# Hashed attention and a two-layer MLP on one core: all queues in a written order from the third chunk on

## The chip, the cores and the metric

The kernel runs on one core of a Trainium2 chip. Times are device microseconds of one execution. A core has five engines with queues of their own: TensorE (PE in the profile, with its weight loads as PEld), VectorE (DVE), ScalarE (ACT), GpSimd (POOL) and SyncE (SP, which here only issues DMAs). An instruction starts when those ahead of it in its queue have gone and when the semaphores it waits for have been raised.

## The reference

Inputs are q, k, v of 4 batches, 8 heads, 768 rows and 64 columns, a projection of 64 x 6, a norm's gain of 512, and two weights of 512 x 2048 and 2048 x 512.

```python
q_bits = einsum('bhsd,dk->bhsk', q, proj) > 0          # 6 bits, k likewise
mask = q_bucket[:, :, :, None] == k_bucket[:, :, None, :]
scores = where(mask, scale * q @ k.T, -1e9)
attn = softmax(scores)                                  # with + 1e-9 in the denominator
x = (attn @ v).transpose(0, 2, 1, 3).reshape(4, 768, 512)
xn = (x - mean) / sqrt(var + 1e-6) * g_ln
out = x + relu(xn @ w_ch1) @ w_ch2
```

## The kernel before

**Chunks.** The output is made in 12 chunks of 256 rows: three for each of four batches, counted here from 0. Chunk n of the loop (line 843) does three things side by side: attention of chunk n, the norm and the first products ("ups", line 559: eight steps of 8 matmuls of 256 columns, L566) of chunk n-1, and the second products ("downs", line 602: eight steps of 4 matmuls of 512 columns, L607) of chunk n-2. Chunks 0 and 1 are in an opening whose order is written out word by word (line 720, `first_two`).

**Attention** of a chunk is 12 units (line 406): four score matmuls (L435), one exponential over 1024 columns on ScalarE (L445), eight value matmuls (L469), and after every third unit a division on VectorE (L487 to L497; from batch 1 on L489, L490, L495, L497). The hash bits are six more rows of the score product, so that unequal buckets fall to nearly nothing.

**MLP.** `norm` (line 532) does statistics and `xn` on VectorE (L516 to L518), then issues from SyncE the DMA that transposes `xn` to `xnT` (L538), then takes the inverse root on GpSimd (L529, L530). In chunk 2 alone `xnT` is made by TensorE and a VectorE copy (`xtrans`, L550, L557). Each up ends with a rectifier, on VectorE and ScalarE in turns (L576, L578). The fourth down of a row block ends with the last sum on VectorE (L612) and the store from SyncE (L616).

**Preparation** of batches 1 to 3 is cut into halves of four heads. A word such as `H20` is step H of batch 2, half 0:

- `L`: loads of q and k (L138, four DMAs on SyncE); `W`: load of v (L157).
- `Q`: four squares on ScalarE for a check of magnitudes (L180), written over the loaded data.
- `N`: q and k to bf16 on GpSimd (L282, two casts into `nat16`, a tile with one buffer).
- `T`: SyncE transposes `nat16` by DMA into `slots` (L304), then moves half of the rows (L309).
- `B`: four block transposes on VectorE (L287) into `bt`; `H`: 32 recorded hash matmuls (L318) that read them, two VectorE instructions (L326, L329), and five DMAs on SyncE (L331, four times L333) that put the bits into `slots`.
- `V`: values to bf16 and their sums, all on GpSimd (L344, L351, L353); `E`: one matmul that shares the sums (L358) and a copy on VectorE (L359).

**What sets the order.** `interleave` (line 678) traces, for each unit, the scores and the exponential of the next unit, then fillers, then the unit's value matmuls and division, then fillers; how many fillers is paid by their costs in the code (a down 870, an up 900, a hash 1300, everything on no PE time 0). In before, the fillers are the norm, the preparation steps of `plan` spread evenly by `mixed` between the downs, then the ups. Only ScalarE keeps this traced order (line 862): for the other four queues Tile's scheduler takes the traced order as a wish, and orders each chunk's instructions by its own priorities and costs. `no_sync_barrier` (line 844) keeps chunks apart in that scheduling.

**Buffers.** PSUM has two banks for the tag `mm`, which ups, downs, hashes, shares and `xtrans` use in turn; two score buffers; two for values. `xn`, `xnT`, `h`, `nat16`, `vnat` and `vs16` have one buffer each.

Of the kernel before, what the change touches and what calls it, by code (L numbers as in the profile page):

```python
# [30 lines left out]
def kernel(  # L31
# [14 lines left out]
    B, H, S, D = q.shape  # L46
# [8 lines left out]
    NT = NC // TT  # L55
# [603 lines left out]

    flag = consts.tile([1, 1], I32)  # L660

    def safety():
        m = work.tile([P, 2], F32, tag="m", name="m")
        nc.vector.tensor_reduce(m, sq, axis=AX.X, op=AOP.max)
        mp = ps_mm.tile([1, 2, P], F32, tag="mm", name="mp")
        for a in range(2):
            nc.tensor.transpose(mp[:, a, :], m[:, a : a + 1], identf)
        m2 = work.tile([1, 2], F32, tag="m2", name="m2")
        nc.vector.tensor_reduce(m2, mp, axis=AX.X, op=AOP.max)
        pr = work.tile([1, 1], F32, tag="pr", name="pr")  # L670
        nc.vector.tensor_mul(pr, m2[:, 0:1], m2[:, 1:2])

        nc.vector.tensor_scalar(
            flag, pr, scalar1=(SAFE_SCORE / scale) ** 2, scalar2=None, op0=AOP.is_le
        )


    def interleave(units, fillers, after=None, single=()):

        total = sum(c for c, _ in fillers) or 1
        slots_n = 2 * len(units)
        done, fi = 0.0, 0

        def fill(upto):
            nonlocal done, fi
            while fi < len(fillers) and done <= upto * total:
                c, f = fillers[fi]
                f()  # L690
                done += c
                fi += 1

        for u, (_, _, values, divide) in enumerate(units):
            nxt = units[u + 1] if u + 1 < len(units) else after
            if nxt:
                nxt[0]()
                nxt[1]()
            fill((2 * u + 1) / slots_n)
            if u % 2 and u // 2 < len(single):  # L700
                for _, f in single[u // 2]:
                    f()
            values()
            divide()
            fill((2 * u + 2) / slots_n)
        while fi < len(fillers):
            fillers[fi][1]()
            fi += 1

    chunks = [(b, t) for b in range(B) for t in range(NT)]  # L710
    preps = [Prep(b) for b in range(B)]
    prep = preps[0]
    def chunk_tile():
        return work.tile([P, TT, d_model], F32, tag="x", bufs=3, name="x")
# [18 lines left out]
    def first_two():  # L733
# [75 lines left out]

    plan = {
        2: "H10 N11 B11 V10 W11 | T11 H11 E10 V11 W20",
        3: "E11 N20 B20 | T20 H20",
        4: "V20 W21 B21 N21 | T21 H21 E20",
        5: "V21 W30 | E21",
        6: "V30 W31 N30 B30 | T30 H30 E30",
        7: "V31 B31 N31 | T31 H31 E31",
    }
    singly = {  # L820
        2: "Q00 L20", 3: "Q01 L21", 4: "Q10 L30", 5: "Q11 L31",
        6: "Q20", 7: "Q21", 8: "Q30", 9: "Q31",
    }

    def prepare(text):
        return [
            step
            for op in text.split()
            for step in preps[int(op[1])].part(op[0], half=int(op[2]))
        ]  # L830

    def mixed(a, b):

        tagged = [((i + 1) / (len(a) + 1), 0, i, s) for i, s in enumerate(a)]
        tagged += [((i + 1) / (len(b) + 1), 1, i, s) for i, s in enumerate(b)]
        return [s for *_, s in sorted(tagged, key=lambda e: e[:3])]

    with tc.manual_schedule():
        first_two()
# [2 lines left out]
    tail = mlp[0][2]  # L842
    for n in range(2, len(chunks)):
        tc.no_sync_barrier()
        mlp[n - 1] = mlp_steps(*chunks[n - 1], xs[n - 1])
        norm, ups, downs, xtrans, _ = mlp[n - 1]
        early, late = (prepare(part) for part in (plan.get(n, "") + "|").split("|")[:2])
        fillers = [norm]
        fillers += mixed(early, tail[:4]) + ([(600, xtrans)] if n == 2 else [])
        fillers += mixed(late, tail[4:]) + ups  # L850
        tail = downs
        if n == NT * (B - 1):
            fillers.append((0, safety))
        after = None
        if n + 1 < len(chunks):
            xs[n + 1] = chunk_tile()
            units[n + 1] = att_units(*chunks[n + 1], xs[n + 1])
            after = units[n + 1][0]
        single = [[step] for step in prepare(singly.get(n, ""))]
        if len(single) > 4:  # L860
            single[3:] = [sum(single[3:], [])]
        with tc.manual_schedule(engines={mybir.EngineType.Activation}):
            interleave(units[n], fillers, after, single)
    tc.no_sync_barrier()
    norm, ups, downs, _, parts = mlp_steps(*chunks[-1], xs[len(chunks) - 1])
# [190 lines left out]
```

## Time and profile before

| what | value |
|---|---|
| median of 3 runs | 321.92 us (320.11 to 322.66) |
| profiled execution, its time | 323.21 us |
| its span, first to last instruction | 320.6 us |
| mean granted TensorE clock | 0.986 |
| PE busy | 304.3 us, 95% of the span |
| ACT, DVE, POOL busy | 216.7, 183.6, 84.8 us |
| chain that ended last | PE 83%, DVE 8%, DMA 4% |

The span is what the trace covers; 2.6 us of the profiled execution's time lie around it. Busy TensorE time counts pipelined matmuls, so 95% doesn't mean that TensorE runs at its peak; the granted clock and the length of like matmuls say more.

### The profile page before, as it was taken

What the parts mean: (1) busy time and instruction counts of PE and PEld (TensorE: products, weight loads), DVE (VectorE), ACT (ScalarE), POOL (GpSimd) and SP (SyncE); (2) the same over time, 40 slices, a digit from 0 to 9 for tenths busy, and PEclk for the clock granted to TensorE, in tenths of its full rate; (3) what the DMA queues carried; (4) which work ended last, traced back from release to release, by engine and by line L of the source; (5) the groups of instructions that cost most, each with busy time, mean ns of one, the idle gap of its engine ahead of it and who ended that gap; (6) DMA issues with size and microseconds to landing.
All of it is one profiled execution on the core that took longest, in us unless ns stands there. A gap on an engine that the chain in (4) does not pass through costs nothing.

```text
span 320.6 us, 7837 instructions
## 1 busy us (share of the span) xinstructions
PE 304.3 (95%) x3268; PEld 227.9 (71%) x3268; DVE 183.6 (57%) x404; ACT 216.7 (68%) x272; POOL 84.8 (26%) x110
## 2 busy tenths in 40 slices
PE   6979999999969997999999999999999999999993
PEld 6566687578648765868868868769769679687563
DVE  1799987634753672465597585535543633635421
ACT  4677976677656674779778778688779667565020
POOL 3467522950330180056064040010200200200200
PEclk9999999999997997999999999999999999999998
DMA  7999996887477489653983533020030110200302
GB/s 241 362 199 302 209 340 103 159 195 197 143 143 215 118 200 177 192 154 133 237 138 90 102 85 86 2 68 34 2 85 15 33 69 0 67 35 0 101 0 76
DMA packets 64970, 40.94 MB, mean 128 GB/s; under 512 B 47152, under 2 KB 59952, under 8 KB 64928
## 3 DMA queue, kind: packets, MB, share of 16 engines
q1 hardware_dynamic: 60224, 31.59, 39.9%
q0 software_dynamic: 4128, 8.13, 10.8%
q10 hardware_dynamic: 576, 0.66, 0.6%
q8 instruction: 27, 0.44, 0.6%
q14 instruction: 15, 0.12, 0.1%
HBM read 27.98 MB, written 6.88 MB: 109 GB/s over the span
## 4 chain that ended last, share of the span: by engine, by line
PE 83%; DVE 8%; DMA 4%; ACT 2%; issue 1%; POOL 0%; SPq 0%; ACTq 0%; POOLq 0%
PE hp L566 27%; PE o L607 21%; PE sc L435 17%; PE av L469 10%; DMA xnT<-xn 3%; PE hash L318 2%; DVE xn L518 2%; DVE slots L262 2%; PE tpose L200 1%; DVE slots L238 1%; DVE bt L287 1%; PE o L589 1%; PE hash L252 1%; DMA knat<-in_k_dram 1%; DVE stats L516 1%
## 5 line engine op out<-in xcount | busy, mean ns | idle before, releaser
L445 ACT ACTIVATE ex<-sc,expb 128x1024 bf16<-128x1024 f32 x144 | 159.4, 1113 | 65.6 <-PE sc L435 63.1
L566 PE MATMUL hp<-xnT,w_sb 128*128 128x256 bf16 x768 | 101.2, 277 | 5.5 <-DMA xnT<-xn 5.2
L607 PE MATMUL o<-w_sb,hbuf 128*128 128x512 bf16 x368 | 92.9, 379 | 0.9 <-DVE x L612 0.8
L435 PE MATMUL sc<-slots 70*128 70x256 bf16 x576 | 87.1, 273 | 2.0 <-POOL slots L238 1.5
L566 PEld LDWEIGHTS <-w_sb 128*128 128x128 bf16 x768 | 72.9, 99 | 15.9 <-DMA xnT<-xn 6.3
L576 DVE TENSOR_SCALAR hbuf<-hp 128x512 bf16<-128x512 f32 x48 | 33.1, 690 | 59.4 <-PE hp L566 59.2
L469 PEld LDWEIGHTS <-ex 128*128 128x128 bf16 x1152 | 54.5, 98 | 15.8 <-ACT ex L445 1.3
L435 PEld LDWEIGHTS <-slots 70*128 70x128 bf16 x576 | 52.0, 97 | 17.1 <-issue 3.7
L469 PE MATMUL av<-vaug,ex 128*128 128x65 bf16 x1152 | 59.3, 194 | 0.3 <-ACT ex L445 0.2
L607 PEld LDWEIGHTS <-hbuf 128*128 128x128 bf16 x368 | 34.0, 97 | 26.8 <-issue 1.1
L529 POOL TENSOR_SCALAR rs<-mv 128x2 f32<-128x2 f32 x12 | 5.6, 471 | 144.2 <-DVE mv L517 144.0
L578 ACT ACTIVATE hbuf<-hp 128x512 bf16<-128x512 f32 x48 | 28.5, 594 | 19.7 <-PE hp L566 19.7
L612 DVE SCALAR_TENSOR_TENSOR x<-o,rs,x 128x512 f32<-128x512 f32 x23 | 17.0, 741 | 31.8 <-PE o L607 31.8
L497 DVE TENSOR_TENSOR x<-x,rc 128x256 f32<-128x256 f32 x36 | 19.0, 528 | 0.9
L282 POOL CAST nat<-qnat 128x1536 bf16<-128x1536 f32 x6 | 9.4, 1570 | 37.5 <-DMA qnat<-in_q_dram 25.5
L518 DVE SCALAR_TENSOR_TENSOR xn<-x,mv,gbc 128x512 bf16<-128x512 f32 x24 | 18.4, 790 | 0.1
L516 DVE BATCH_NORM_STATS2 stats<-x 128x6 f32<-128x512 f32 x24 | 15.4, 681 | 0.3
L490 DVE TENSOR_TENSOR x<-av,vsum 128x256 f32<-128x256 f32 x36 | 14.9, 414 | 0.0
L489 DVE TENSOR_SCALAR rc<-av 128x4 f32<-128x4 f32 x36 | 5.7, 157 | 15.7 <-PE av L469 15.7
L344 POOL CAST vaug<-vnat 128x1536 bf16<-128x1536 f32 x8 | 11.9, 1493 | 7.6 <-PE av L469 4.0
L180 ACT ACTIVATE knat<-knat 128x768 f32<-128x768 f32 x16 | 13.4, 835 | 0.0
L180 ACT ACTIVATE qnat<-qnat 128x768 f32<-128x768 f32 x16 | 13.3, 833 | 0.0
(86 smaller groups left out, 219.8 us busy)
## 6 DMA issues: line engine op xcount, KB each, us to landing
out_dram<-x SPq DMA_DIRECT2D x23, 256.0 KB
vnat<-in_v_dram SPq DMA_DIRECT2D x7, 768.0 KB
qnat<-in_q_dram SPq DMA_DIRECT2D x11, 384.0 KB
knat<-in_k_dram SPq DMA_DIRECT2D x11, 384.0 KB
w_sb<-in_moe_w_ch_dram POOLq DMA_DIRECT2D x4, 1024.0 KB, 14.2
slots<-slots SPq DMA_DIRECT2D x6, 384.0 KB
qnat<-in_q_dram POOLq DMA_DIRECT2D x2, 768.0 KB, 14.7
knat<-in_k_dram POOLq DMA_DIRECT2D x2, 768.0 KB, 16.0
```

The source lines that it names most:

```text
L180: nc.scalar.activation(src, src, AF.Square, accum_out=sq[:, a, col : col + 1],)
L435: nc.tensor.matmul(sc[:, i, :], key_block(h, kj), query_blocks(h),)
L445: nc.scalar.activation(ex, sc, AF.Exp, bias=expb[:, 1:2] if b else expb[:, 0:1], scale=scale if b else scale / Q_SCALE,)
L469: nc.tensor.matmul(av[:, h - ha, qi, :], state[g][:, i, qi * P : (qi + 1) * P], va[:, h, kj, :], start=(b > 0 and (g, i, qi) == (0, 0, 0)) ...
L497: nc.vector.tensor_tensor(xv, num, rc.unsqueeze(3).to_broadcast([P, 2, TT, D]), op=AOP.mult)
L516: nc.vector.bn_stats(stats, x[:, i, :])
L518: nc.vector.scalar_tensor_tensor(xn[:, :, i, :], x[:, i, :].rearrange("p (o d) -> p o d", d=P), mv[:, i, 0:1], gbc.rearrange("p (o d) -> p ...
L566: nc.tensor.matmul(hp[:, i, :], w1_sb[:, dt, nt * P : (nt + 1) * P], st["xnT"][:, dt, :], start=(dt == 0), stop=(dt == ND - 1),)
L576: nc.vector.tensor_scalar_max(dst, src, 0.0)
L578: nc.scalar.activation(dst, src, AF.Relu)
L607: nc.tensor.matmul(o2, st["h"][:, nt, i * P : (i + 1) * P], w2_sb[:, nt, :], start=(nt == 0), stop=(nt == NH - 1),)
L612: nc.vector.scalar_tensor_tensor(x[:, i, :], o2, st["rs"][:, i : i + 1], x[:, i, :], op0=AOP.mult, op1=AOP.add,)
```

## The change

The diff replaces `plan` and `mixed` by `steps`, one string for each of chunks 2 to 8 and 10; other chunks use `plain`. In a string `n` is the norm, `d` and `u` are the next down and the next up, `x` is `xtrans`; each `N` or `B` stands for one of the two casts or four block transposes, and other words for whole preparation steps. The check of magnitudes (`safety`) is cut in two, `m` and `s`, and goes from the end of chunk 9 into chunk 10. And `manual_schedule()` without a list of engines makes all five queues keep the traced order.

```diff
-    plan = {
-        2: "H10 N11 B11 V10 W11 | T11 H11 E10 V11 W20",
-        3: "E11 N20 B20 | T20 H20",
-        4: "V20 W21 B21 N21 | T21 H21 E20",
-        5: "V21 W30 | E21",
-        6: "V30 W31 N30 B30 | T30 H30 E30",
-        7: "V31 B31 N31 | T31 H31 E31",
-    }
+    steps = {
+        2: "n d d H10 d d x N11 d N11 d T11 V10 d W11 d B11 u B11 u B11 u B11 u H11 u E10 u V11 u u",
+        3: "n d d d N20 d N20 B20 E11 d T20 d B20 W20 d d B20 u B20 u H20 u u u u u u",
+        4: "n d d d N21 d N21 B21 d T21 d B21 d d B21 u B21 V20 u H21 u u u W21 u u u",
+        5: "n d d d E20 V21 d d d d d u u u W30 u u E21 u u u",
+        6: "n d d d N30 d N30 B30 d T30 d B30 d d B30 u B30 V30 u H30 u u u W31 u u u",
+        7: "n d d d N31 d N31 B31 E30 d T31 d B31 d d B31 u B31 V31 u H31 u u u u u u",
+        8: "n d d d E31 d d d d d u u u u u u u u",
+        10: "n d d d d m d d d d u u u s u u u u u",
+    }
+    plain = "n d d d d d d d d u u u u u u u u"
...
+    def sequence(text, norm, downs, ups, xtrans):
...
-        fillers = [norm]
-        fillers += mixed(early, tail[:4]) + ([(600, xtrans)] if n == 2 else [])
-        fillers += mixed(late, tail[4:]) + ups
+        fillers = sequence(steps.get(n, plain), norm, tail, ups, xtrans)
...
-        with tc.manual_schedule(engines={mybir.EngineType.Activation}):
+        with tc.manual_schedule():
             interleave(units[n], fillers, after, single)
```

The words of `singly` (squares `Q` and loads `L`) stay between the units where they were. After the loop the last norm, downs and ups are traced as before.

More of the change, by code (lines that the diff above doesn't have):

```diff
@@ L660, with row_maxima, safety @@
     flag = consts.tile([1, 1], I32)
-    def safety():
+    def row_maxima():
         m = work.tile([P, 2], F32, tag="m", name="m")
         nc.vector.tensor_reduce(m, sq, axis=AX.X, op=AOP.max)
+        return m
+    def safety(m):
         mp = ps_mm.tile([1, 2, P], F32, tag="mm", name="mp")
@@ L823, with prepare @@
     }
[L825 to L836, printed above, removed]
+    parts_left = {}
+    def prepare(op):
+        kind, b, half = op[0], int(op[1]), int(op[2])
+        return preps[b].part(kind, half)
+    def sequence(text, norm, downs, ups, xtrans):
+        downs, ups, out = list(downs), list(ups), []
+        for word in text.split():
+            if word == "n":
+                out.append(norm)
+            elif word == "d":
+                out.append(downs.pop(0))
+            elif word == "u":
+                out.append(ups.pop(0))
+            elif word == "x":
+                out.append((600, xtrans))
+            elif word == "m":
+                out.append((0, lambda: parts_left.__setitem__("m", row_maxima())))
+            elif word == "s":
+                out.append((100, lambda: safety(parts_left["m"])))
+            elif word[0] in "BN":
+                if word not in parts_left:
+                    parts_left[word] = prepare(word)
+                out.append(parts_left[word].pop(0))
+            else:
+                out += prepare(word)
+        assert not downs and not ups
+        return out
     with tc.manual_schedule():
@@ L846 @@
         norm, ups, downs, xtrans, _ = mlp[n - 1]
-        early, late = (prepare(part) for part in (plan.get(n, "") + "|").split("|")[:2])
-        fillers = [norm]
-        fillers += mixed(early, tail[:4]) + ([(600, xtrans)] if n == 2 else [])
-        fillers += mixed(late, tail[4:]) + ups
+        fillers = sequence(steps.get(n, plain), norm, tail, ups, xtrans)
         tail = downs
-        if n == NT * (B - 1):
-            fillers.append((0, safety))
         after = None
@@ L858 @@
             after = units[n + 1][0]
-        single = [[step] for step in prepare(singly.get(n, ""))]
+        single = [[step] for op in singly.get(n, "").split() for step in prepare(op)]
         if len(single) > 4:
             single[3:] = [sum(single[3:], [])]
-        with tc.manual_schedule(engines={mybir.EngineType.Activation}):
+        with tc.manual_schedule():
             interleave(units[n], fillers, after, single)
```

## The prediction

> **What bounds the kernel now.** I read the page first: TensorE is busy 95% of the span and is 83% of the chain that ended last. So only two things can move the time: moments in which TensorE waits, and stretches in which it runs slower. The busy time cut at the chunks' borders (a chunk begins with the scores of its second unit) shows where these are. Columns: length, then busy us and instruction counts of PE, PEld, DVE, ACT, POOL, then the granted clock, the DMA share, GB/s. Rows are chunks 2 to 7.
>
> ```profile
> 51.80:79.00 27.20, 26.41 (x319) 19.71 (x317) 15.60 (x28) 18.48 (x25) 14.05 (x16) 1.00 0.69 155
> 79.00:107.80 28.80, 25.84 (x280) 19.00 (x277) 14.93 (x33) 18.35 (x25) 7.46 (x7) 0.94 0.60 155
> 107.80:135.40 27.60, 25.60 (x278) 18.81 (x275) 15.76 (x35) 18.41 (x25) 7.48 (x9) 0.94 0.80 188
> 135.40:157.70 22.30, 22.30 (x248) 17.14 (x245) 12.79 (x29) 18.19 (x25) 9.92 (x11) 1.00 0.56 179
> 157.70:181.50 23.80, 23.80 (x279) 17.95 (x276) 17.53 (x35) 18.32 (x25) 9.10 (x10) 1.00 0.75 131
> 181.50:205.30 23.80, 23.80 (x279) 17.95 (x275) 15.22 (x35) 18.32 (x25) 3.28 (x5) 1.00 0.26 58
> ```
>
> From chunk 5 on TensorE never stops and the clock is 1.00: 22.3 us, and 23.8 with a hash (1.44 us) and a share (0.1). Chunks 3 and 4 hold that same work and take 28.8 and 27.6, at a clock of 0.94. Who TensorE waited for (total, times, longest):
>
> ```profile
> PE hp L566 <- DMA xnT<-xn: 5.2, 3, 2.9
> PE o L607 <- DVE x L612: 0.8, 1, 0.8
> ```
>
> The first is the first up waiting for its transposed input, in chunk 3, in chunk 4 and at the kernel's end. The second falls in chunk 2. Why `xnT` is late stands in SyncE's own order (start, length):
>
> ```profile
> 88.52 3.71 SPq L304 DMA_TRANSPOSE slots<-nat  x1
> 92.34 1.26 SPq L538 DMA_TRANSPOSE xnT<-xn  x1
> ...
> 114.86 3.67 SPq L304 DMA_TRANSPOSE slots<-nat  x1
> 118.63 1.26 SPq L538 DMA_TRANSPOSE xnT<-xn  x1
> ```
>
> `xn` of chunk 3 was done at 83.8 (L518, 83.07 + 0.74), but the scheduler put `T20` ahead of it, and `T20` waited for the GpSimd casts until 88.5 and held the queue until 92.2. TensorE then shows the price twice:
>
> ```profile
> 95.45 1.05 PE L566 MATMUL hp<-xnT,w_sb 128*128 128x256 bf16 x8 [2.88 <-DMA xnT<-xn]
> 96.33 0.41 PE L469 MATMUL av<-vaug,ex 128*128 128x65 bf16 x8
> 96.58 0.74 PE L435 MATMUL sc<-slots 70*128 70x256 bf16 x4
> 97.11 1.92 PE L566 MATMUL hp<-xnT,w_sb 128*128 128x256 bf16 x8
> ```
>
> A wait of 2.88 us, and then an up of 1.92 instead of 1.04: after each of the two waits the granted clock drops for a few us. The wait of 0.80 in chunk 2 is followed by full speed. So a short wait costs itself, a long one about 1.7 us more (chunk 3 loses 5.0 with 2.9 of wait; chunk 4 loses 3.8 with 2.0; the excess is 2.1 and 1.8, part of it issue).
>
> **The change, queue by queue.** In chunks 8 to 11 the traced order of before already is what TensorE ran, so nothing changes there except `safety`.
>
> *SyncE.* `n` comes first, so `xnT` leaves ahead of `T`, of the bits' five DMAs and of the loads. Chunk 5 shows what such an order gives: its first down starts at 135.85, L538 at 139.56, its first up at 146.56, without a wait. From issue to the first up that read it took 3.1 us in chunk 3 (92.34 to 95.45), so 3.9 us are spare. What now stands behind `xnT` (`T` 3.7, L309 0.7 after its landing, five bit DMAs 0.4 + 3.05 and their landing, the stores 0.4 each, four loads 0.5 each) feeds the slots and values of the next batch or half, which are wanted half a chunk later or more. In chunk 2, `H11` is after the loads `L20`; its bits are wanted by unit 6 of chunk 3, some 9 us into it, and I count them there by about 82 us of the span against 88. Gain: 28.8 - 23.8 = 5.0 in chunk 3, 27.6 - 23.8 = 3.8 in chunk 4. Both are whole, wait and clock.
>
> *VectorE, chunk 2.* The 0.80 came from the last sum L612 behind four block transposes (4 x 0.9). These go behind the downs, so L612 follows its down. Gain 0.8.
>
> *Hashes (`H20`, `H21`, `H30`, `H31`).* Each moves from the downs to behind the second up. Its matmuls cost the same 1.44 wherever they are. But the last two block transposes move too, and in VectorE's fixed order the fourth is behind a rectifier and a division. From the end of the last down TensorE reaches the hash after 0.44 + 0.87 + 0.25 + 0.44 + 0.87 + 0.25 = 3.1 us, and after half of the hash, at 3.9, needs the fourth transpose. VectorE is there after 0.2 (release: in chunk 5 a down's values follow it at 140.68, L612 starts at 140.88) + 0.63 (L612 to the next start, 115.18 to 115.81) + 0.89 (third transpose) + 0.63 (rectifier) + 1.03 (division, 101.55 to 102.58) + 0.94 (fourth) = 4.3. So a new wait of 0.4. No row of before has it; below it is 0 if VectorE runs ahead, above it is 1.6 by the longest L497 seen, 1.635 instead of 0.42:
>
> ```profile
> 166.28 1.58 DVE L497 TENSOR_TENSOR x<-x,rc 128x256 f32<-128x256 f32 x1
> ```
>
> That one lay beside a GpSimd cast from 166.13 to 167.59, and `V` (cast 1.5, sums 3.3) runs in this place in chunks 4, 6 and 7, though GpSimd starts it early, behind the casts of `N`. I take 0.55 each, near the lower end: 4 x 0.55 = 2.2 lost. What is late next is the second score block behind it; ScalarE has 1.4 us of hash to catch up in.
>
> [...]
>
> *Shares.* In chunks 3 and 7 a share stands between the last down of one row block and the first of the next. It takes the second `mm` bank, so the down must wait for L612 to empty the first: 0.2 + 0.75 after the fourth down, less 0.36 of values and share, 0.6. Nearest row: the 0.80 above. Bounds 0 and 0.8; I take 0.65 x 2 = 1.3.
>
> *The rest at nothing.* `N`, `V`, `W`, `E20`, `E21` and `V31` go later. GpSimd is busy for 7.5 us in chunk 3 and idle for up to 20.7 us at a time (the longest wait of L529), which hides them; their results are for the batch after. Without that cover a late `N` only delays `T`, no longer `xnT`. If a load lands late, VectorE's `B` blocks what is behind it; before, `L20` was issued at 77.5 and its third piece landed at 85.5; now it goes from about 70, when its last square is done, so there are 5 us to spare. `m` and `s` (two transposes of TensorE, 0.38, and four small VectorE instructions) only change place; uncovered they cost some 1 us (0.38 and four of about 0.16, as L495 takes). Each queue holds as many instructions as before.
>
> *Sum.* 5.0 + 3.8 + 0.8 - 2.2 - 1.3 = 6.1 us. Of the profiled execution: span 320.6 to 314.5, time 323.2 to 317.1. The median of the runs is 1.3 below that execution: **315.8 us**.
>
> **Rivals.**
> (a) *No new wait.* VectorE and the banks keep up: 321.9 - 9.6 = 312.3. For it: VectorE is busy only 15 to 17 of 24 us. Against it: the two orders above.
> (b) *SyncE is late again.* Loads now come late in a chunk, just ahead of the next `xnT`. For it: `T30`, issued right behind loads, held SyncE for 7.39 us instead of 3.7, as much as the spare 3.9. Against it: I count the loads out by the time the norm is done. If half of the 8.8 comes back: 321.9 - 0.8 - 4.4 + 3.5 = 320.2.
> (c) *Slower: hash behind VectorE.* Same place as my 0.55, but divisions or rectifiers wait for GpSimd casts and sums and each hash waits 1.6 or more, with the clock drop of 1.7: 4 x 3.3 = 13.2, and 321.9 - 9.6 + 13.2 + 1.3 = 326.8. It decides from 2.1 us per hash on (8.3 in four), which needs the drop. For it: the 1.58 row, a fixed order. Against it: waits up to 0.8 show no drop, and `V` should mostly be over by then.
> [...]
> (d) *It doesn't do what it says*: some order stays or a wait of another kind eats it; 321.9.
>
> **How the numbers follow.** Forecast 0.50, (a) 0.18, (b) 0.09, (c) 0.17, (d) 0.06. A measurement of this kernel tells about 1%, 3.2 us, from no change. Faster by more (under 318.7): forecast and (a), with a little of the forecast's tail moved over, 0.67. Within 1%: (b), (d) and that tail, 0.16. Slower: (c), 0.17. The range runs from 312.0, just under (a), over the forecast's own ends (0 to 1.0 per hash, 0 to 0.8 per share: 312.3 to 317.9), (b) and (d), to 322.5; only most of (c) is out.
>
> **What would show it.** Right: chunks 3 and 4 at 24 to 25 us with clock 1.00; L538 within 4 us of each chunk's start and ahead of L304; TensorE's waits for `xnT` only the last 0.35; waits of half a microsecond of L318 for L287 and of L607 for L612. Wrong: a wait of 2 us or more anywhere from chunk 2 to 7 with the clock below 1.00, above all at L318, or L566 still waiting for L538.

## The result and the profile after

The changed kernel is slower: 325.86 us median against 321.72 of the kernel before (20 runs each), ratio 1.0119 with a 95% interval of 1.0086 to 1.0153. (The ratio leaves out runs more than 1.5% above the quickest of their kernel, so it isn't quite the quotient of the medians.) The profiled execution of after took 322.48 us, span 319.8, 3.4 us under its median; that of before lay 1.5 us above its own. So the two traces differ by a gain of 0.8 us in span, where the medians differ by a loss of 4.1. The trace of after shows one stall of the kind that costs the time; what fills the other 3.4 us of the median is in no trace of the changed kernel.

Busy time by chunk of that execution, chunks 2 to 7, columns as before:

```profile
52.50:78.78 26.28, 26.12 (x316) 19.77 (x317) 15.40 (x28) 18.48 (x25) 9.20 (x11) 1.00 0.55 124
78.78:103.65 24.87, 24.43 (x277) 18.26 (x276) 16.87 (x33) 18.04 (x25) 9.20 (x10) 1.00 0.69 179
103.65:128.59 24.94, 24.24 (x276) 18.02 (x275) 16.06 (x34) 18.15 (x25) 9.16 (x10) 1.00 0.70 151
128.59:155.35 26.76, 24.25 (x246) 18.20 (x245) 12.01 (x30) 18.37 (x25) 6.21 (x8) 0.94 0.67 201
155.35:179.59 24.24, 24.09 (x276) 18.10 (x275) 15.61 (x34) 18.04 (x25) 9.19 (x10) 1.00 0.43 98
179.59:204.53 24.94, 24.28 (x277) 18.21 (x276) 17.14 (x35) 18.04 (x25) 9.19 (x10) 1.00 0.52 119
```

Chunks 2, 3 and 4 gained 0.9, 3.9 and 2.7 us, chunks 6 and 7 lost 0.4 and 1.1: about as forecast. Chunk 5, which took 22.3 without a stop in before, takes 26.8 at a clock of 0.94, 4.5 us more. What TensorE waited for:

```profile
PE hp L566 <- DMA xnT<-xn: 3.2, 3, 2.3
PE o L607 <- DVE x L612: 0.9, 2, 0.6
```

The wait for `xnT` was not removed; it moved from chunks 3 and 4 to chunk 5 (2.35 us there, 0.59 left in chunk 4). SyncE's order ahead of it:

```profile
124.53 1.59 SPq L331 DMA_DIRECT2D bits_d<-bits  x1
128.58 3.06 SPq L333 DMA_DIRECT2D slots<-bits_d  x4
131.74 0.44 SPq L138 DMA_DIRECT2D qnat<-in_q_dram  x1
132.29 0.40 SPq L138 DMA_DIRECT2D knat<-in_k_dram  x1
132.74 1.45 SPq L138 DMA_DIRECT2D qnat<-in_q_dram  x1
134.25 0.47 SPq L138 DMA_DIRECT2D knat<-in_k_dram  x1
134.81 0.41 SPq L157 DMA_DIRECT2D vnat<-in_v_dram  x1
135.33 2.44 SPq L538 DMA_TRANSPOSE xnT<-xn  x1
```

`xnT` does come ahead of `T` now. But the loads written at the end of chunk 4 stand behind L333, which waits for the bits to land in DRAM (issued at 124.53, read back from 128.58). So five loads, 2.3 MB, leave just when `xn` is done (133.2), and the transpose leaves 2.1 us late and takes until 142.26 to be of use, 6.9 us instead of the 3.1 of chunk 3 before.

### The profile page after: what moved, and what is told of

It reads as the page before. It is cut to its first block, busy times and chain, and to the rows that moved or that the text cites. A ratio compares the mean times of both kernels' runs of the same rounds, so it can differ in the third digit from the quotient of the medians.

```text
span 319.8 us, 7815 instructions
## 1 busy us (share of the span) xinstructions
PE 304.4 (95%) x3245; PEld 228.8 (72%) x3268; DVE 187.5 (59%) x404; ACT 215.9 (68%) x272; POOL 84.8 (27%) x110
## 4 chain that ended last, share of the span: by engine, by line
PE 81%; DVE 9%; DMA 6%; issue 1%; ACT 1%; POOL 0%; SPq 0%; DVEq 0%; POOLq 0%
PE hp L566 27%; PE o L607 20%; PE sc L435 17%; PE av L469 10%; DMA xnT<-xn 5%; PE hash L318 3%; DVE slots L238 3%; DVE slots L262 2%; PE tpose L200 1%; PE o L589 1%; DMA knat<-in_k_dram 1%; DVE xn L518 1%; DVE stats L516 1%; DVE x L497 1%; PE hash L252 1%
## 5 line engine op out<-in xcount | busy, mean ns | idle before, releaser
L566 PE MATMUL hp<-xnT,w_sb 128*128 128x256 bf16 x768 | 99.7, 274 | 3.5 <-DMA xnT<-xn 3.2
L607 PE MATMUL o<-w_sb,hbuf 128*128 128x512 bf16 x345 | 90.7, 379 | 1.8 <-DVE x L612 0.9
L529 POOL TENSOR_SCALAR rs<-mv 128x2 f32<-128x2 f32 x12 | 8.6, 713 | 168.9 <-DVE mv L517 168.8
L612 DVE SCALAR_TENSOR_TENSOR x<-o,rs,x 128x512 f32<-128x512 f32 x23 | 17.3, 751 | 41.0 <-PE o L607 36.1
L497 DVE TENSOR_TENSOR x<-x,rc 128x256 f32<-128x256 f32 x36 | 18.2, 506 | 1.2
L516 DVE BATCH_NORM_STATS2 stats<-x 128x6 f32<-128x512 f32 x24 | 16.5, 691 | 0.4
L353 POOL TENSOR_TENSOR vsum<-vsum,vaug 128x256 f32<-128x256 f32 x18 | 12.5, 697 | 1.4
```

The source lines that it names most:

```text
L497: nc.vector.tensor_tensor(xv, num, rc.unsqueeze(3).to_broadcast([P, 2, TT, D]), op=AOP.mult)
L516: nc.vector.bn_stats(stats, x[:, i, :])
L566: nc.tensor.matmul(hp[:, i, :], w1_sb[:, dt, nt * P : (nt + 1) * P], st["xnT"][:, dt, :], start=(dt == 0), stop=(dt == ND - 1),)
L607: nc.tensor.matmul(o2, st["h"][:, nt, i * P : (i + 1) * P], w2_sb[:, nt, :], start=(nt == 0), stop=(nt == NH - 1),)
L612: nc.vector.scalar_tensor_tensor(x[:, i, :], o2, st["rs"][:, i : i + 1], x[:, i, :], op0=AOP.mult, op1=AOP.add,)
```

## The experiments

Theory S: the loss is SyncE's fixed order, which holds loads and `xnT` behind waits. Theory V: it is VectorE's fixed order, which holds hashes and shares. Ratios are to the kernel before, run in the same rounds as the experiment; e1 to e4 were timed together, so were e5 to e8 and e9 to e11.

**e1, the changed kernel again.**

> The changed kernel itself, for a second profile: its first profiled execution (322.5 us) is one of its quickest, 3.4 us under its median. Theory S (SyncE's queue: the loads of batch 3 and of the values stand just ahead of chunk 5's xnT, which then lands 2.35 us late and costs 4.5 us with the clock drop): the typical execution has this wait longer, or a second one of the kind in chunk 4, where 0.59 us was seen. Theory V (VectorE's fixed order: hashes wait for block transposes, shares for the last sum): the typical execution has longer waits of L318 for L287, over 1 us each. Time 325.5 by both.

324.99 us, ratio 1.0112 (1.0074 to 1.0150). The profiled execution, 321.78, was the quickest of ten and showed the same 2.35 us in chunk 5, none in chunk 4. Its mean clock was 0.991; in seven of the other nine executions it was 0.985 or 0.986, which would fit one more stretch of some 3.2 us at half clock (0.005 x 320 x 2), so one more TensorE wait as long as the 2.00 to 2.88 us ahead of the drops in the traces of before and after. That is not shown, and it can't be all: another execution here took 324.97 us at 0.995, and in the 20 runs above the median clock was 0.989, with 325.57 and 327.00 us at 0.994. e2, e5 and e6 have waits for `xnT` in chunk 3, so that is a likely place for a part of the loss.

**e2, L30 behind the next chunk's `xnT`.**

```diff
-        2: "Q00 L20", 3: "Q01 L21", 4: "Q10 L30", 5: "Q11 L31",
+        2: "Q00 L20", 3: "Q01 L21", 4: "Q10", 5: "Q11 L31",
-        5: "n d d d E20 V21 d d d d d u u u W30 u u E21 u u u",
+        5: "n d d d E20 V21 d d L30 d d d u u u W30 u u E21 u u u",
```

> The changed kernel with the loads L30 moved from unit 7 of chunk 4 to chunk 5, behind its second row block's first down, so that 1.5 MB fewer stand ahead of chunk 5's xnT in SyncE's queue. Theory S: L566's wait for xnT in chunk 5 falls from 2.35 to under 0.3 us and the clock stays at 1.00 there; 4 to 5 us quicker than the changed kernel, 321. Theory V: no change, 325.5 within 1.5.

318.35 us, ratio 0.9932 (0.9888 to 0.9976). Chunk 5's wait is 0.28 and its clock full (the mean of the execution is 0.996, against 0.991 in e1). Moving four DMA instructions takes back 6.6 us, more than S had said.

**e3, the new sequence, only ScalarE held.**

```diff
-        with tc.manual_schedule():
+        with tc.manual_schedule(engines={mybir.EngineType.Activation}):
             interleave(units[n], fillers, after, single)
```

> The changed kernel's new sequence, but only ScalarE held to it as before the change; the other four queues are ordered by Tile's scheduler. Theory S: the scheduler again puts slots transposes ahead of xnT in some chunk, so waits like those of before, 321 to 324. Theory V: without the fixed VectorE order the hash and share waits go, and with N and T written later xnT goes first: 316 to 319.

320.02 us, ratio 0.9939 (0.9903 to 0.9975): between the two. `xnT` waits fell to 0.84 at most, but the scheduler let downs wait for L612 three times (4.5 us in all). So the new sequence as a wish is a small gain, 1.4 us; holding every queue to it costs 5 us on top.

**e4, the old plan, all queues held.**

```diff
-        with tc.manual_schedule(engines={mybir.EngineType.Activation}):
+        with tc.manual_schedule():
             interleave(units[n], fillers, after, single)
```

> The kernel before with its old plan, but all five queues held to the traced order. Hashes are among the downs there, ahead of the divisions that delay them, and the loads come earlier in their chunk. Theory S: xnT first in every chunk, loads out in time, so no xnT wait over 0.5 us; 316 to 318. Theory V: the four block transposes stand ahead of the last sum and of the divisions, downs and values wait for VectorE; 322 or more.

329.70 us, ratio 1.0288 (1.0205 to 1.0371). S was right that `xnT` would no longer be waited for (0.21 us, at the kernel's end), and wrong on the time, which V had. VectorE, then TensorE in chunk 3:

```profile
82.85 0.42 DVE L359 COPY vsum<-share 128x256 f32<-128x256 f32 x1
90.37 0.98 DVE L287 STREAM_TRANSPOSE bt<-qnat 128x768 f32<-128x768 f32 x1 [7.10 <-DMA qnat<-in_q_dram]
```

```profile
94.94 2.46 PE L318 MATMUL hash<-bt,proj 128*32 128x192 f32 x24 [6.18 <-DVE x L612]
```

A block transpose that waits for its load holds all of VectorE for 7.1 us, and a hash then TensorE for 6.2. The load itself left late: SyncE sent it at 83.83, behind L333 (79.62), where before had sent it at 77.51. So a held VectorE passes on what a held SyncE delays, and can be as dear; the changed kernel writes `B` late enough to escape that.

**e5, the block transposes early, the shares later.**

```diff
-        6: "n d d d N30 d N30 B30 d T30 d B30 d d B30 u B30 V30 u H30 ...
+        6: "n d d d N30 d N30 B30 d T30 d B30 B30 d B30 d u V30 u H30 ...
-        7: "n d d d N31 d N31 B31 E30 d T31 d B31 d d B31 u B31 V31 u H31 ...
+        7: "n d d d N31 d N31 B31 d T31 E30 d B31 B31 d B31 d u V31 u H31 ...
```

(3 and 4 likewise.)

> The changed kernel with VectorE's part of the order mended: the last two block transposes of H20, H21, H30, H31 ahead of the eighth down instead of behind it (so ahead of the rectifier and the division), and the shares E11 and E30 behind a row block's first down instead of just ahead of it. Theory V: what the change lost is here; the hash waits (0.4 to 0.5 us each) and the share waits (0.3 to 0.55) go, 2.5 us or more quicker than the changed kernel, 322.5 or less. Theory S: those 2.5 us go at most, the late xnT stays, so still 322 to 324 and half clock in chunk 5.

325.13 us, ratio 1.0140 (1.0057 to 1.0224): no gain. In its trace every hash runs its 1.51 us without a stop and the share waits are gone, yet

```profile
PE hp L566 <- DMA xnT<-xn: 8.8, 4, 5.6
```

What TensorE saved, it then waited for SyncE, 5.56 us in chunk 5. V's waits are real, but taking them away doesn't help while SyncE is held.

**e6, the bits of `H11` ahead of `L20`.**

```diff
-        2: "... B11 u H11 u E10 u V11 u u",
+        2: "... B11 u H11 L20 u E10 u V11 u u",
```

with `L20` taken out of `singly`.

> The changed kernel with the loads L20 behind the bit DMAs of H11 instead of ahead of them in SyncE's queue, chunk 2. Theory S: in chunk 3 SyncE is held by L333, which waits 6 to 8 us for the bits' way through DRAM behind 1.5 MB of loads; with the loads behind, L333 goes at about 76 instead of 84 us, xnT of chunk 3 leaves at 82 instead of 87, and a wait there of 0 to 0.8 us goes; but L20 itself and all that follows from it (N20, T20) come 8 us later, so chunk 5's wait stays: 322 to 326. Theory V: no change, 325.

325.74 us, ratio 1.0161 (1.0095 to 1.0227). L333 went at 80.06 instead of 83.62, but four loads then stood between it and `xnT`, which waited 1.84 us in chunk 3, 3.96 in chunk 4 and not in chunk 5. The stall follows the loads: S had the time right, but had put the wait in chunk 5.

**e7, SyncE alone left to the scheduler.** The other four queues are held to the changed kernel's order; in the two traces VectorE, ScalarE and GpSimd run the same instructions in the same order.

```diff
-        with tc.manual_schedule():
+        with tc.manual_schedule(engines={mybir.EngineType.Activation, mybir.EngineType.PE, mybir.EngineType.DVE, mybir.EngineType.Pool}):
```

> The changed kernel with SyncE's queue alone left to Tile's scheduler; PE, DVE, ACT and POOL keep exactly the changed order. In SyncE's queue the scheduler puts loads between a hash's write of its bits (L331) and the reads back (L333), which wait for it, and T ahead of the bits' reads. Theory S: the loss is in SyncE's fixed order alone, so 4 to 7 us quicker than the changed kernel, 318 to 321, with hash and share waits as they were. Theory V: SyncE's order doesn't matter; 325.

317.01 us, ratio 0.9899 (0.9833 to 0.9965): 4.6 us under before in these rounds, where the changed kernel lay 4.1 over it in its own, and quicker than S had said. No wait for `xnT` is left from chunk 3 on but one of 0.22 us at the kernel's end; the hash and share waits are as they were. Chunk 5, then SyncE near it:

```profile
127.40:150.00 22.60, 22.54 (x247) 17.21 (x244) 11.95 (x30) 18.21 (x25) 6.22 (x8) 1.00 0.55 162
```

```profile
120.00 2.33 SPq L138 DMA_DIRECT2D qnat<-in_q_dram  x2
122.42 0.46 SPq L331 DMA_DIRECT2D bits_d<-bits  x1
122.98 0.38 SPq L138 DMA_DIRECT2D knat<-in_k_dram  x1
127.17 3.04 SPq L333 DMA_DIRECT2D slots<-bits_d  x4
130.26 0.50 SPq L138 DMA_DIRECT2D knat<-in_k_dram  x1
132.22 1.29 SPq L538 DMA_TRANSPOSE xnT<-xn  x1
134.49 0.38 SPq L157 DMA_DIRECT2D vnat<-in_v_dram  x1
```

L333 still starts 4.8 us behind L331 (4.1 in after), but three of four loads go ahead of it, the load of v goes behind `xnT`, and the transpose takes 1.29 us to issue. With one queue's order changed, the loss is gone and most of the forecast gain is there: the cause lies in the order of one queue that computes nothing.

**e8, the reverse: ScalarE and SyncE held, the rest free.**

```diff
-        with tc.manual_schedule():
+        with tc.manual_schedule(engines={mybir.EngineType.Activation, mybir.EngineType.SP}):
```

> The changed kernel with only ScalarE and SyncE held to the traced order; PE, DVE and POOL ordered by Tile's scheduler. Theory S: the late xnT of chunk 5 with its clock drop stays, 322 to 326. Theory V: as with all but ScalarE free (320.0), 319 to 321.

326.36 us, ratio 1.0187 (1.0098 to 1.0276), against 320.02 and 0.9939 with SyncE free too (e3).

```profile
PE hp L566 <- DMA xnT<-xn: 4.2, 3, 3.2
```

Holding SyncE brings a loss of the same size back, but by another path. The longest wait, 3.17 us with a clock drop (the mean clock of the execution is 0.994, against 0.998 in e3), is in chunk 4, and there SyncE sent `xnT` as soon as `xn` was done (116.1). It was `xn` that was late: the scheduler had put two block transposes between the steps of the norm on VectorE, and these waited 2.75 and 1.67 us for loads that SyncE had sent only at 106.97, behind L333. In e3 the first of them had gone at 93.98.

**e9, the reads of the bits from GpSimd's queue.**

```diff
-                nc.sync.dma_start(
+                nc.gpsimd.dma_start(
                     out=self.sl[D:K1, 4 * half + g].rearrange(
```

> The changed kernel with the four reads of the bits (L333) issued from GpSimd's queue instead of SyncE's. GpSimd then waits for the bits' write to land, and SyncE is free for what is behind: loads and xnT. Theory S1 (SyncE is held by L333's wait, 5 to 8 us per hash, and by its 3 us of issue): the loads of chunks 3 and 4 and xnT leave 5 to 8 us earlier, xnT waits go, 317 to 320. Theory S2 (it is the bytes of the loads just ahead of xnT, not the held queue): the order of loads and xnT is the same, so the wait in chunk 5 stays, 323 to 326.

332.81 us, ratio 1.0357 (1.0304 to 1.0410): slower than either theory gave, by another queue:

```profile
POOL slots L333 <- DMA bits_d<-bits: 61.0, 6, 15.8
```

```profile
PE share L358 <- POOL vs L353: 13.8, 1, 13.8
```

GpSimd, held by the same wait, kept back the value sums of `V11`, and the share `E11` stopped TensorE for 13.8 us. TensorE never waited for `xnT` for 0.15 us or more in chunks 3 to 10, though the loads stand ahead of it as in the changed kernel. In chunk 5 the five loads had left at 136.67 to 139.77 and `xnT` followed at 148.24, 8.5 us behind the last. That speaks for the held queue (S1), which sends the loads late, rather than for the bytes alone (S2); but chunk 3 was so much longer here that it is no clean test, and how much of the loss each makes stays open.

**e10, all held, loads written behind the next `xnT`.**

```diff
+        3: "n d d L20 d d d E11 W20 d d d u u u u u u u u",
+        4: "n d d L21 d N20 d N20 B20 d T20 B20 d B20 d B20 d u u H20 V20 u u u u u u",
+        5: "n d d L30 d N21 d N21 B21 d E20 T21 W21 B21 d B21 d B21 d u u H21 u u V21 u u u u",
+        6: "n d d L31 d N30 d N30 B30 d E21 T30 B30 d B30 d B30 d u u H30 W30 u u u u u u",
...
```

More than the loads moves here: `N`, `B`, `T`, `H`, `V`, `W` and `E` of batches 2 and 3 follow up to a chunk later, and block transposes and shares change place as in e5.

> All five queues held as in the changed kernel, but a sequence written anew for SyncE: each load L goes into the next chunk, behind its xnT, and N, B, T, H, V, W, E of batches 2 and 3 follow up to a chunk later; the last two block transposes stand ahead of the eighth down and the shares behind a row block's first down. Theory S: no xnT wait over 0.4 us but the last one, no clock drop, no hash and share waits: chunks 3 to 7 at 22.3 to 24 us, 313 to 316, quicker than before and than all runs so far. Theory V: 322 or more, since VectorE's order is held as tightly as in the changed kernel.

317.76 us, ratio 0.9900 (0.9848 to 0.9952). A written order can do it too, but it stayed above the 313 to 316 that S gave: SyncE's next hold-up made `E21` wait 1.61 us in chunk 6 and `xnT` 1.37 in chunk 7, since `T` behind four loads took 7 us to issue.

**e11, e5's order with SyncE free.**

> The kernel with the block transposes early and the shares later (e5), with SyncE's queue left to Tile's scheduler (as e7). Theory S with V as the small term: e7's 317.0 less the hash and share waits that were left there (4 times 0.4 to 0.5, 0.5 and 0.55, so 2.5 to 3), 314 to 315. Were the two terms not additive (hash waits gave SyncE the time that it needs): 316 to 318, with an xnT wait back in chunk 3 or 5.

315.66 us, ratio 0.9831 (0.9793 to 0.9870): the best of all, 5.1 us under before in its rounds and some 9 to 10 under the changed kernel. Its chunks 3 to 7:

```profile
79.30:103.30 24.00, 23.86 (x277) 18.11 (x276) 16.27 (x33) 18.04 (x25) 4.33 (x4) 1.00 0.69 184
103.30:127.40 24.10, 23.79 (x277) 18.03 (x276) 16.66 (x34) 18.07 (x25) 9.17 (x10) 1.00 0.77 187
127.40:150.00 22.60, 22.44 (x246) 17.21 (x245) 11.94 (x30) 18.22 (x25) 6.22 (x8) 1.00 0.56 163
150.00:173.70 23.70, 23.59 (x276) 17.99 (x275) 15.72 (x34) 18.04 (x25) 9.19 (x10) 1.00 0.51 122
173.70:198.10 24.40, 23.87 (x277) 18.11 (x276) 16.99 (x35) 18.15 (x25) 9.19 (x10) 1.00 0.43 90
```

The same edit of VectorE's order that gave nothing in e5 seems to give something here. The chunks above are 2.0 us shorter in sum than e7's in the profiled executions, and every hash takes 1.51 us; the median is 1.35 under e7's, of the 2.5 expected. But the two were run in different rounds and their intervals overlap, so the size is not settled. The profiled execution lost 1.0 us in its opening against e7's.

## Why the prediction was wrong

- **`xnT` ahead of `T`, 5.0 and 3.8 us: right in place and kind.** Chunk 3 lost its wait whole: 28.80 to 24.87, with the new small waits 3.9 against 3.8 in the sum. Chunk 4 gave 2.7 against 3.2; 0.59 of wait stayed.
- **Chunk 2, 0.8: right**, 0.9.
- **Hashes, 4 x 0.55: right.** The hashes wait for block transposes (L287), as counted; they took 1.93, 1.99, 2.05 and 1.92 us instead of 1.51, 1.9 in sum against 2.2. In chunk 3:

```profile
93.11 1.93 PE L318 MATMUL hash<-bt,proj 128*32 128x192 f32 x32
```

- **Shares, 2 x 0.65: right in kind, too large**; the waits were 0.33 and 0.55.
- **The step that failed is SyncE's paragraph.** It took "3.9 us are spare" from chunk 5 of before, where the scheduler had sent the last load at 132.41, 7.1 us ahead of `xnT`, and "L538 within 4 us of each chunk's start" from the same row. In after it left 8.0, 5.2 and 6.7 us after the start of chunks 3, 4 and 5. The stretch behind `xnT` was costed by its issue times, with the landings named but not added to the loads behind them. They were most of it. SyncE's waits for the landings in after, then in before:

```profile
SPq L309 <- DMA slots<-nat: 17.3, 6, 3.9
SPq L333 <- DMA bits_d<-bits: 17.3, 6, 6.0
```

```profile
SPq L333 <- DMA bits_d<-bits: 7.4, 4, 4.4
SPq L309 <- DMA slots<-nat: 6.2, 3, 3.9
```

In before the scheduler had put stores and loads into these gaps. So "from about 70" for the loads `L20` became 74.41, "the bits by about 82" became L333 at 83.62 to 86.65, and "loads out by the time the norm is done", the argument against rival (b), was untrue. In chunk 5 `xnT` left 2.1 us late and, right behind the loads, took 3.8 us longer than the 3.1 assumed. Spare were 3.6 us there (`xn` done at 133.2, the first up due at 139.9, less 3.1); they were used up, and the remaining 2.35 are the wait; with the clock drop chunk 5 lost 4.5. Without this step the sum was near: with SyncE free (e7) the same order took 317.01 us, against 315.8.
- **Rival (b) was the right mechanism**, with a chance of 0.09 and a price of 320.2. Both came from that same count. It let half of the old loss come back, 4.4 us. That the profiled execution lost 4.5 in chunk 5 is luck: it is a new loss, in a chunk that had none. In the median some 9 us came back (325.86 against e7's 317.01).
- **Rival (c)** had the right sign and the wrong place: no hash waited over 0.6 us.
- The range ended at 322.5 since (b) was bounded by what before had lost. Nothing bounds it so: in e5 the waits for `xnT` came to 8.8 us, and chunk 5 alone took 31.0 us in place of 22.3.

## What to carry to other kernels

A queue that only issues DMAs can bound a kernel as an engine does (here SyncE's order alone stands between the ratios 1.0119 and 0.9899): when its order is fixed, add up each DMA's wait for the landing that it needs, not its issue time, and ask what stands behind it. A round trip through DRAM (write, wait, read back: 2.6 to 6.6 us from L331 to L333 in after) in such a queue wants independent transfers between its two halves, and a transfer on the critical path wants to be written ahead of loads that are not. Hold the queues whose order you have counted, and leave the others to the scheduler: here four held queues and a free SyncE made 317.01 us with the new sequence, and 315.66 with VectorE's part of it mended.

## What the runs showed of the hardware

The clock drop doesn't follow from the length of a wait alone. TensorE waits of 2.88 and 2.00 us (before, chunks 3 and 4) and 2.35 (after, chunk 5) were followed by half clock (by slices of 1 us the granted clock is 0.50 from 97 to 100 and from 125 to 127 us in before, and from 144 to 146 in after); waits of 2.17 (e5, chunk 3) and 2.29 (e4, chunk 5) were not, nor was one of 1.84 (e6, chunk 3): the granted clock of these three chunks is 1.00. The rows of e5 for chunks 3 and 5, with waits of 2.17 and 5.56:

```profile
78.40:104.50 26.10, 23.93 (x278) 17.97 (x275) 15.80 (x33) 18.10 (x25) 9.24 (x10) 1.00 0.67 172
129.20:160.20 31.00, 25.38 (x246) 18.69 (x243) 12.02 (x30) 18.31 (x25) 6.21 (x8) 0.89 0.60 171
```

0.11 of 31.0 us is 6.8 us at half clock, and 0.06 of 26.76 in after's chunk 5 is 3.2. By slices of 0.5 us, each of the three drops in before and after named above comes to 3.4 us at half clock; e5's chunk 5 has about twice that. Why a wait of 2.00 us was followed by a drop and one of 2.17 was not is not shown: no run here moves one wait alone.
